# Pooled attention and an eight-expert layer on one core: padded head pairs, values stationary, tokens gathered to expert slots inside SBUF

## The chip, the cores and the metric

One core of a Trainium2 chip runs the whole program. The metric is device time in microseconds (us), the median of several executions. Profiles are of one execution; their times count from the start of its span. All comparisons below use runs of the state "fast" unless a text says otherwise. Engines: PE does matmuls, DVE and ACT are the vector and scalar engines, POOL is the general engine that also gathers and issues casting and indirect DMAs, SP issues plain DMAs.

## The reference, cut to what matters

```python
# q, k, v: (8 batches, 8 heads, 1152, 64) fp32
q_pool = q.reshape(B, H, S // 2, 2, D).mean(axis=3)            # 576 queries per head
attn   = softmax(1 / sqrt(D) * q_pool @ k.T)                   # 576 x 1152 per head
x      = (attn @ v).transpose(0, 2, 1, 3).reshape(4608, 512)   # 4608 tokens
for e in range(8):                                             # each token has one expert
    m = domain_id == e
    out[m] = maximum(x[m] @ w1[e], 0) @ w2[e]                  # 512 -> 1024 -> 512
```

## The kernel before

Heads are done one after the other. Per chunk of 128 keys the scores come out with keys on partitions, go through the exponential, and each 128x128 block of exponentials is then loaded as *weights*, past which 65 columns of values (64 and a column of ones for the softmax sum) are moved. Tokens go to a slot buffer in DRAM (`x_slot`) by indirect DMA and are read back per expert. The listing is shortened, with numbers put in for names.

```python
for c in range(NC + 1):                      # 9 key chunks, software pipelined
    ...
    nc.tensor.matmul(sA, lhsT=klhs, rhs=qrhs[:, 0:320])          # 64 rows
    nc.tensor.matmul(oja[:, 0, :], lhsT=attnT[:, cp, 0:P], rhs=v16[:, cp, :])   # 65 columns
    nc.tensor.matmul(sB, lhsT=klhs, rhs=qrhs[:, 320:576])
    ...
    nc.scalar.activation(attnT[:, c, 0:320], sA, AF.Exp, scale=0.0625)          # L317
    nc.scalar.activation(attnT[:, c, 320:576], sB, AF.Exp, scale=0.0625)        # L318
for jj in range(2, NJ):                      # 27 late value matmuls per head, L323
    for c in range(NC):
        nc.tensor.matmul(tps, lhsT=attnT[:, c, jj*P : jj*P+rows], rhs=v16[:, c, :], ...)
# normalise with ACT (scale = 1/sum) into xrow, then scatter rows to x_slot in DRAM
...
for e in range(E):                           # experts, after all attention
    for tt in range(6):                      # 768 slots per expert
        ...                                  # load 128 tokens, transpose, two layers, scatter
```

The softmax here doesn't subtract the row's maximum and nothing guards it: scores larger than these inputs give would overflow.

## Time and profile before

960.9 us median (960.5 to 962.8, 4 runs).

| stretch of the profile (span 954.4 us) | what happens | granted clock |
|---|---|---|
| 0 to 676 us | attention, a steady head 10.1 us | page: 1.00 to 103 us, then 0.50 (see below) |
| 676 to 697 us | no matmul: the last rows go to DRAM and back | 0.5 |
| 697 to 954 us | experts | about 0.9, with falls to 0.5 |

The first fence has whole lines of the page's head: busy time of each engine with its share of the span, then busy tenths in 40 slices and the granted PE clock in tenths.

```profile
span 954.4 us, 19171 instructions
PE 874.5 (92%) x6793; PEld 457.4 (48%) x6793; DVE 412.6 (43%) x2058; ACT 614.3 (64%) x1916; POOL 151.0 (16%) x183
...
PE   5699999999999999999999999999278898889896
...
ACT  3577677677677776777677776776245655665553
...
PEclk9999655555555555555555555555578998999899
```

PE looks full all through attention, at half the clock. The 1.00 of the first 103 us is no reading: the trace has no clock record before 100.8 us, and sA and sB start 0.24 us apart at 86 us as at 115 us. The groups of instructions (line, engine, operation, shapes, count | busy us, mean ns | idle time of the engine before them and who ended it) show what ACT does there and what it waits for:

```profile
L317 ACT ACTIVATE attnT<-sA 128x320 f16<-128x320 f32 x576 | 254.5, 442 | 164.2 <-PE sA L295 145.6
L318 ACT ACTIVATE attnT<-sB 128x256 f16<-128x256 f32 x576 | 220.7, 384 | 18.2 <-PE sB L307 14.6
L295 PE MATMUL sA<-qT,kT 64*128 64x320 f16 x576 | 226.8, 442 | 0.7 <-ACT attnT L317 0.5
```

The 475 us of exponentials are a floor of that design; ACT idles another 182 us in front of them, mostly for PE, while PE does the late value matmuls, transposes and first scores of the next head. The timeline inside a head shows the two exponentials back to back (start in us, duration in us, instruction, then in brackets the idle time before it and who ended it):

```profile
307.15 0.44 ACT L317 ACTIVATE attnT<-sA 128x320 f16<-128x320 f32 x1 [0.22 <-PE sA L295]
307.49 0.38 ACT L318 ACTIVATE attnT<-sB 128x256 f16<-128x256 f32 x1
```

### The profile page before, as it was taken

The page shows a single profiled execution, that of the slowest core. Times are in us where ns is not written, and L with a number is a line of the kernel's source. Part 1 is how long each engine was busy: PE and PEld are TensorE (multiplying, and loading weights), DVE is VectorE, ACT ScalarE, POOL GpSimd, SP SyncE. Part 2 cuts the span into 40 slices and gives each one's busy share as a digit, 9 for nine tenths or more (in the row PEclk, how much of TensorE's full clock was granted, in tenths as well). Part 3 has the DMA queues.
Part 4 walks back from the last instruction along what each step waited for, and adds up shares of the span by engine and source line. Part 5 has one row for each costly group of instructions (what it writes and reads, how often), then busy time and mean ns, then how long its engine had stood idle before and what let it go on. Part 6 is the DMA issues. An engine that isn't in the chain of part 4 may idle for free. (4 is left out here: it accounts for less than half of the span.)

```text
span 954.4 us, 19171 instructions
## 1 busy us (share of the span) xinstructions
PE 874.5 (92%) x6793; PEld 457.4 (48%) x6793; DVE 412.6 (43%) x2058; ACT 614.3 (64%) x1916; POOL 151.0 (16%) x183
## 2 busy tenths in 40 slices
PE   5699999999999999999999999999278898889896
PEld 1344544444444444444444444444155565556563
DVE  5455554554555554554554554543022312231221
ACT  3577677677677776777677776776245655665553
POOL 8322232220010001002000100200211211221221
PEclk9999655555555555555555555555578998999899
DMA  9964454444345344355363543440025466556221
GB/s 307 302 111 92 97 116 99 95 125 97 79 128 158 82 102 115 91 165 123 77 169 86 121 106 82 120 132 1 25 73 169 155 211 217 163 178 220 64 66 40
DMA packets 230244, 118.31 MB, mean 124 GB/s; under 512 B 169818, under 2 KB 212866, under 8 KB 230148
## 3 DMA queue, kind: packets, MB, share of 16 engines
q1 hardware_dynamic: 221028, 96.61, 38.7%
q0 software_dynamic: 9120, 20.48, 5.9%
q8 instruction: 53, 0.87, 0.4%
q14 instruction: 43, 0.35, 0.1%
HBM read 96.53 MB, written 23.64 MB: 126 GB/s over the span
## 5 line engine op out<-in xcount | busy, mean ns | idle before, releaser
L317 ACT ACTIVATE attnT<-sA 128x320 f16<-128x320 f32 x576 | 254.5, 442 | 164.2 <-PE sA L295 145.6
L318 ACT ACTIVATE attnT<-sB 128x256 f16<-128x256 f32 x576 | 220.7, 384 | 18.2 <-PE sB L307 14.6
L295 PE MATMUL sA<-qT,kT 64*128 64x320 f16 x576 | 226.8, 442 | 0.7 <-ACT attnT L317 0.5
L307 PE MATMUL sB<-qT,kT 64*128 64x256 f16 x576 | 207.2, 406 | 1.5 <-ACT attnT L318 1.1
L265 DVE CAST kT<-tr 128x128 f16<-128x128 f32 (+1 forms) x320 | 85.6, 284 | 178.2 <-PE sB L307 139.2
L405 PE MATMUL hps<-xT,w1h 128*128 128x128 f16 x1536 | 132.7, 228 | 20.6 <-ACT hT L412 13.5
L412 ACT ACTIVATE hT<-hps 128x128 f16<-128x128 f32 x384 | 94.8, 278 | 74.5 <-PE hps L405 71.0
L405 PEld LDWEIGHTS <-w1h 128*128 128x128 f16 x1536 | 110.9, 102 | 62.2 <-issue 55.5
L400 DVE CAST xT<-tpx 128x128 f16<-128x128 f32 x192 | 50.0, 287 | 172.7 <-PE tpx L393 163.2
L298 PEld LDWEIGHTS <-attnT 128*128 128x128 f16 x576 | 56.4, 115 | 132.5 <-ACT attnT L318 113.2
L415 PE MATMUL o_ps<-w2h,hT 128*128 128x512 f16 x384 | 112.8, 397 | 0.0
L323 PEld LDWEIGHTS <-attnT 128*128 128x128 f16 (+1 forms) x1728 | 104.8, 141 | 6.0
L279 DVE CAST qT<-tr 128x128 f16<-128x128 f32 (+1 forms) x320 | 81.5, 271 | 28.9 <-PE tr L272 21.6
L424 POOL DMA_INDIRECT out_dram<-osb,gt x48 | 48.9, 1018 | 207.1 <-ACT hT L412 105.1
L272 PE MATMUL tr<-ident_63,qpa 128*128 128x128 f16 (+1 forms) x320 | 76.2, 269 | 2.0 <-DVE qpa L233 0.6
L295 PEld LDWEIGHTS <-kT 64*128 64x128 f16 x576 | 51.5, 100 | 53.2 <-issue 12.5
L336 DVE RECIPROCAL rec<-oja 128x1 f32<-128x1 f32 (+1 forms) x192 | 30.1, 157 | 105.4 <-PE oja L323 103.8
L309 PEld LDWEIGHTS <-attnT 128*128 128x128 f16 x576 | 60.8, 122 | 21.9 <-PE sA L295 18.7
L227 DVE TENSOR_TENSOR qpa<-q2a 128x64 f16<-128x64 f32 (+1 forms) x320 | 68.9, 215 | 2.2 <-DMA q2a<-in_q_dram 1.9
L307 PEld LDWEIGHTS <-kT 64*128 64x128 f16 x576 | 55.5, 108 | 27.9 <-issue 13.1
L233 DVE TENSOR_TENSOR qpa<-q2a 128x64 f16<-128x64 f32 (+1 forms) x320 | 68.7, 215 | 0.0
L337 ACT ACTIVATE xrow<-oja,rec 128x64 f16<-128x64 f32 (+1 forms) x192 | 61.3, 319 | 3.3 <-DVE rec L336 3.1
(774 smaller groups left out, 939.2 us busy)
## 6 DMA issues: line engine op xcount, KB each, us to landing
w_sb<-in_moe_w_dram SPq DMA_DIRECT2D x16, 2048.0 KB
k_sb<-in_k_dram SPq DMA_DIRECT2D x64, 288.0 KB
v_sb<-in_v_dram SPq DMA_DIRECT2D x64, 288.0 KB
q2a<-in_q_dram SPq DMA_DIRECT2D x256, 64.0 KB
x_slot<-xz_115 POOLq DMA_DIRECT2D x48, 128.0 KB, 4.3
q2a<-in_q_dram SPq DMA_DIRECT2D x64, 32.0 KB
gt<-g_slot SPq DMA_DIRECT2D x48, 0.5 KB
out_dram<-osb,gt POOLq DMA_INDIRECT x48, 2.7
```

Of the source, the lines that this page charges most:

```text
L227: nc.vector.tensor_tensor(out=qpa[0:rows, jj, 0:D], in0=q2a[0:rows, jj, 0:D], in1=q2a[0:rows, jj, D : 2 * D], op=ALU.add,)
L265: nc.vector.tensor_copy(kT[0 : nch * D, p_, :], tps[0 : nch * D, :])
L272: nc.tensor.matmul(tq[:, 0:rows], lhsT=qpa[0:rows, jj, :], rhs=ident16[0:rows, 0:rows], start=True, stop=True,)
L279: nc.vector.tensor_copy(qT[:, jj * P : jj * P + rows], tq[:, 0:rows])
L295: nc.tensor.matmul(sA[:, :], lhsT=klhs, rhs=qrhs[:, 0:NA], start=True, stop=True)
L307: nc.tensor.matmul(sB[:, :], lhsT=klhs, rhs=qrhs[:, NA:Sp], start=True, stop=True)
L317: nc.scalar.activation(attnT[:, c, 0:NA], sA[:, :], AF.Exp, bias=0.0, scale=0.0625)
L318: nc.scalar.activation(attnT[:, c, NA:Sp], sB[:, :], AF.Exp, bias=0.0, scale=0.0625)
L323: nc.tensor.matmul(tps[0:rows, tslot, :], lhsT=attnT[:, c, jj * P : jj * P + rows], rhs=v16[:, c, :], start=(c == 0), stop=(c == NC - 1),)
L405: nc.tensor.matmul(hps[:, :], lhsT=w1h[:, c, f * P : (f + 1) * P], rhs=xT[:, c, :], start=(c == 0), stop=(c == NDc - 1),)
L412: nc.scalar.activation(hT[:, f, :], hps[:, :], AF.Relu)
L415: nc.tensor.matmul(o_ps[:, :], lhsT=hT[:, f, :], rhs=w2h[:, f, :], start=(f == 0), stop=(f == NF - 1),)
```

## The change

The intent: make PE work dense so that the exponentials are the only limit of attention, fill PE's spare time with expert work, and keep tokens inside SBUF.

- Two heads form a pair. Keys of both lie on 128 partitions; the queries of each head are padded with zeros in the other head's 64 rows, so each score matmul has 128 rows.
- Values are the stationary operand, exponentials move (288 columns at a time). The output comes out transposed, x on partitions, ready for the first expert layer. One exponential covers both heads: 576 steps of 576 columns.
- The sums go out by DMA, are inverted, and come back broadcast over partitions; two DVE multiplies per pair normalise into `xT`, 4 channel groups of a token side by side.
- POOL gathers tokens of an expert from `xT` in SBUF (`indirect_copy`). 256 slots per expert ("fill", 128 units on PE, first-half tokens only) run inside the second half of attention, 384 more per expert in a last stage.
- All instruction streams are in an order set by hand.

The diff is a rewrite (746 lines against 461); its core:

```diff
-            nc.tensor.matmul(sA[:, :], lhsT=klhs, rhs=qrhs[:, 0:NA], ...)
-            nc.tensor.matmul(oja[0:P, 0, :], lhsT=attnT[:, cp, 0:P], rhs=v16[:, cp, :], ...)
-            nc.scalar.activation(attnT[:, c, 0:NA], sA[:, :], AF.Exp, bias=0.0, scale=0.0625)
-            nc.scalar.activation(attnT[:, c, NA:Sp], sB[:, :], AF.Exp, bias=0.0, scale=0.0625)
+        for r in range(2):                                   # score(t): step t = (pair, half, chunk)
+            mm(s[:, r, 0:QH], kq[p][:, c * P : (c + 1) * P],
+               qz[p % 2][r][:, hf * QH : (hf + 1) * QH], True, True)
+        nc.scalar.activation(e_[:, :, :], st.pop(t)[:, :, 0:QH], AF.Exp, bias=0.0, scale=0.0625)
+        for head in range(2):                                # av_step(t)
+            mm(acc[u][head][:, 0:QH], v16[p % NV][:, c, P * head : P * head + P],
+               e_[:, head, :], c == 0, c == NC - 1)
+    def norm_c(p, hh):                                       # L469
+        nc.vector.tensor_tensor(
+            out=xT[lo : lo + 64, 1 + b * Sp : 1 + (b + 1) * Sp, hp].rearrange("p (a j) -> p j a", j=NJ),
+            in0=xu[p][hh][lo : lo + 64, :].rearrange("p (j a) -> p j a", j=NJ),
+            in1=srec[p][lo : lo + 64, :].rearrange("p (j a) -> p j a", j=NJ), op=ALU.mult)
+        nc.gpsimd.indirect_copy(                             # gather, L320: 128 tokens x 4 values
+            xs[:, :, j * P : (j + 1) * P].rearrange("p c s -> p s c"),
+            xT[:, 0:hi, :], idx[:, e, t * 8 : (t + 1) * 8], True)
 ... (cut)
+        if main and hf == 0 and c == 0 and p >= 1 and p + 1 < NPAIR:
+            pair_load(p + 1)                                 # k, v by POOL (cast), q by SP
+            if hf == 0 and c == 0:
+                prep_k(p + 1)                                # DVE: kp
+            if hf == 0 and c == 2:
+                burst_k(p + 1)                               # PE: 8 transposes of kp
+            if hf == 1 and c == 6:
+                norm_c(p - 1, 0)
+            if hf == 1 and c == 7:
+                norm_c(p - 1, 1)
```

A pair has 18 steps: two halves (hf) of nine chunks (c).

## The prediction

> **What bounds it now.** The table by stretches shows attention to about 676 us, a 20 us gap without matmuls, experts from 697 to 954. A head takes 10.1 us (oja matmuls): 9 x (442 + 384) ns = 7.4 us is the two exponentials per key chunk, back to back in the timeline; for the other 2.7 us ACT mostly idles (164 us before L317, 146 on PE) while PE does 27 late value matmuls with new weights (1.7 us), transposes and first scores. PE is 100% busy, yet the granted clock is 0.50 from 103 to 700 us. Before that the page says 1.00, but 64x320 matmuls take 442 ns there too, so I read half clock throughout. In the expert stage (0.9 to 1.0) a 128x512 matmul starts every 0.215 us. The Trainium skill ("TensorE: Matmul & The Clock Gate", part 1) has 1.2 GHz idle, 2.4 GHz after sustained activity; this trace shows that a full PE queue of 64-row scores and 65-column value matmuls did not suffice, and that 128x128 expert work raised the clock within about 8 us.
>
> **What changes.** Values become the weights and exp(scores) moves: 576 steps, each two score matmuls (128 rows, half zeros) and two value matmuls of 288 columns, one exponential of 576 columns. Gone: 2880 attnT weight loads, 320 xrow copies (104 us ACT), the x_slot round trip, 8 w2 casts on ACT (29 us). Added: about 40% of the expert work (128 units of 1024 columns) inside attention, 40 gathers and the cast-DMA issues on POOL, a normalisation round trip per pair.
>
> **Costs** (estimates from the trace).
> - Exponential: 0.9 ns per column from 442 and 384 ns, so 576 columns 655 to 670 ns; x576 = 380 us, the floor of attention.
> - PE at full clock, columns/2.4 GHz: 0.49 us per step, transposes about 0.07, a fill unit 0.44. 432 steps without fill are ACT bound, with bursts about 0.70 us: 303. 144 steps with fill are PE bound, about 1.0 us: 145.
> - Dense 128-row work should raise the clock; before's experts kept it at about 68% column activity (8704 columns per 5.3 us tile), the new ACT-bound steps have about 75%.
> - Start 12 us; gap before the tail (normalise, three gathers) 18.
> - Tail: 24,576 columns per expert, 10.3 us. POOL issues three gathers, three scatters (1.0 us each, as before) and for four experts four weight DMAs. No gather is in this trace; I take 2 to 3 us. Then POOL is slightly the limit: 8 x 12 = 96. End 6.
>
> Sum 580; median 585 us, 80% range 530 to 710; faster 0.97, same 0.01, slower 0.02.
>
> **Right if:** ACT over 90% busy until the fill, an exponential about 0.66 us; PEclk near 1.0 from the first tens of us; step time 1.0 us in the fill; PE at 80 to 95% in the tail.
>
> **Wrong if:**
> 1. The clock stays at 0.5 in attention: steps PE bound at 1.05 and 1.9 us, total 750 to 850.
> 2. Gathers are slow. The skill ("GPSIMD Engine Reference", section 7) has about 102 cycles for a small read command per gather index; 128 of them would be an estimated 11 us, 22 us per expert in the fill and 35 in the tail: over 800 us, POOL near 100%.
> 3. PE order makes ACT wait at transposes or late weights.
> 4. DVE, some 13 us per pair in the fill, delays the two shared PSUM buffers.

## The result, and the profile after

906.9 us median (904.3 to 908.9, 4 runs) against 960.9 us. The ratio is 0.943, 95% interval 0.9415 to 0.9453. Ratios in this document are the mean time of one kernel's fast runs over that of the other's of the same rounds, so not quite the ratio of the medians quoted. Faster, by 6% and not by the 39% predicted; the time lies far outside the range.

Names in the views that follow: `s` holds scores, `e` their exponentials, `accA` and `accB` the accumulators of the two heads, `xuA` and `xuB` their copies in SBUF before normalising, `rb` the inverse sums, `kp` the copied keys of the next pair, `mt` the PSUM tile of transposes and fill, `xs` gathered tokens.

The head of the page after. DVE and POOL are given as well here, as they turn out to matter:

```profile
span 902.1 us, 10215 instructions
PE 555.1 (62%) x3619; PEld 360.5 (40%) x3619; DVE 461.9 (51%) x680; ACT 384.9 (43%) x625; POOL 285.2 (32%) x316
...
PE   4787567765786768358358557676860555343555
...
DVE  6867375675767546466465666567662111000111
ACT  3777456745576644135134334674760111100111
POOL 2588210110000042351351331200001456554443
PEclk9999888968798778688687778898895786667887
```

Work fell as planned: PE from 875 to 555 us, ACT from 614 to 385. But no engine is full any more; each waits for others. The groups:

```profile
L420 ACT ACTIVATE e<-s 128x576 f16<-128x576 f32 x576 | 358.6, 650 | 310.0 <-PE s L402 304.0
...
L320 POOL INDIRECT_COPY xs<-xT,idx 128x512 f16 x40 | 112.9, 2823 | 254.1 <-issue 220.4
...
L469 DVE TENSOR_TENSOR xT<-xuA,rb 64x576 f16<-64x576 f32 x32 | 110.1, 3440 | 38.1 <-DMA rb<-s_rec 38.1
...
L469 DVE TENSOR_TENSOR xT<-xuB,rb 64x576 f16<-64x576 f32 x32 | 89.5, 2796 | 1.0
```

One exponential takes 650 ns, close to the 655 to 670 predicted. ACT idles 310 us before them, more than before. Two more things stand out: a multiply of only 576 columns costs 2.8 us, and the gathers have twice as much "issue" before them (220 us) as work (113 us).

The sum of the prediction against the profile. A step is put down to its exponential; the fill is taken as 144 steps from the 313th on, as predicted (in b1, where it starts 12 steps later, from the 325th).

| stretch | predicted us | after, us | with all mends (b1, below), us |
|---|---|---|---|
| start, to the first exponential | 12 | 14.5 | 14.5 |
| 432 steps without fill | 303 | 407.0 | 306.1 |
| 144 steps with fill | 145 | 249.1 | 155.7 |
| last exponential to first matmul of the last stage | 18 | 37.3 | 25.3 |
| last stage and end | 102 | 194.2 | 147.0 |
| sum | 580 | 902.1 | 648.6 |

**A pair without fill** takes 16 to 17 us where it is steady, for 18 x 0.62 = 11.1 us of exponentials. The timeline of DVE around the border of two pairs:

```profile
253.74 2.79 DVE L469 TENSOR_TENSOR xT<-xuA,rb 64x576 f16<-64x576 f32 x1 [0.17 <-DMA rb<-s_rec]
256.56 2.79 DVE L469 TENSOR_TENSOR xT<-xuB,rb 64x576 f16<-64x576 f32 x1
259.38 0.81 DVE L368 COPY kp<-k 128x576 f16<-128x576 f16 x2
260.23 0.46 DVE L443 COPY xuA<-accA 128x288 f32<-128x288 f32 x1
```

and of PE and ACT at the same time:

```profile
256.27 0.29 PE L402 MATMUL accB<-e,v 128*128 128x288 f16 x1
256.39 0.41 PE L402 MATMUL s<-qz,kq 128*128 128x288 f16 x2
260.25 0.62 PE L376 MATMUL mt<-ident,kp 128*128 128x128 f16 x8 [3.45 <-DVE kp L368]
...
261.10 0.45 PE L402 MATMUL accA<-e,v 128*128 128x288 f16 x1
261.34 0.45 PE L402 MATMUL accB<-e,v 128*128 128x288 f16 x1
```

```profile
247.00 10.55 ACT L420 ACTIVATE e<-s 128x576 f16<-128x576 f32 x17 [0.31 <-PE s L402]
261.41 0.65 ACT L420 ACTIVATE e<-s 128x576 f16<-128x576 f32 x1 [3.86 <-PE s L402]
```

Seventeen exponentials run back to back in 10.55 us. Then PE stands at the eight key transposes (L376) for `kp`, which DVE makes only after both multiplies. Scores behind the transposes in PE's order come late, and ACT stops for 3.9 us. A second loss follows: matmuls of 288 columns start 0.12 us apart before the stall and 0.24 us after it, until about 264 us; the clock record has 0.50 from 260.8 to 264.2 us. Each of these steps shows ACT idle 0.31 us. The Trainium skill ("TensorE: Matmul & The Clock Gate", "Why this matters for your kernels") says that idle gaps above about 3 us between bursts send the clock back to half; the trace agrees, with a gap of 3.45 us. Of its 35 falls to half clock, all but the last, at the program's end, have a gap of 3.19 us or more in the 7 us before. It is no sharp bound: in run e7 below, 8 of 22 falls had only gaps of 1.9 to 2.8 us there.

**In the fill**, a pair takes up to 34 us. POOL's timeline there:

```profile
489.99 2.77 POOL L320 INDIRECT_COPY xs<-xT,idx 128x512 f16 x1 [4.21 <-PE s L402]
498.59 2.78 POOL L320 INDIRECT_COPY xs<-xT,idx 128x512 f16 x1 [5.83 <-issue]
500.90 0.84 POOL L90 DMA_DIRECT2D k<-in_k_dram  x1
```

The key load of the next pair stands behind two gathers in POOL's order; it lands at 504.9, and ACT is idle from 496.9 to 507.4 us. ACT's stops in the fill are 6.5 to 16.2 us long. The gathers and the multiplies also slow each other: the multiply that starts at 492.57 us takes 6.28 us in place of 2.79, and these two gathers are 8.6 us apart in place of 6.5. Here it is the part of the gather shown as issue that grows (5.83 us in place of 3.7); the second multiply, beside the part shown as work, keeps its 2.79 us. The skill ("GPSIMD Engine Reference", section 8, "Key points") says that the two engines share SBUF interfaces and that DVE instructions with two SBUF inputs contend; the multiply is one, and the trace agrees.

**In the last stage** an expert takes 26.6 us with weight loads in POOL's order, 23.5 without; PE is busy half of it. One expert on POOL:

```profile
738.14 2.80 POOL L320 INDIRECT_COPY xs<-xT,idx 128x512 f16 x1 [4.15 <-issue]
744.66 2.80 POOL L320 INDIRECT_COPY xs<-xT,idx 128x512 f16 x1 [3.72 <-issue]
751.15 2.82 POOL L320 INDIRECT_COPY xs<-xT,idx 128x512 f16 x1 [3.68 <-issue]
```

Gathers follow each other every 6.5 us although each shows only 2.8 us of work. The 3.7 us of "issue" between them are the engine's own. The skill ("Perfetto Trace Analysis", "GPSIMD Engine Instruction") says that the start shown for such an instruction is a read on its first core and not the start of execution, which fits. Three gathers (19.5 us), three scatters with their memsets (4.0) and four weight issues (3.0) fill the 26.6 us.

### The profile page after: what moved, and what is told of

It is laid out like the page before. It is cut to its first block, busy times and chain, and to the rows that moved or that the text cites. A ratio compares the mean times of both kernels' runs of the same rounds, so it can differ in the third digit from the quotient of the medians.

```text
span 902.1 us, 10215 instructions
## 1 busy us (share of the span) xinstructions
PE 555.1 (62%) x3619; PEld 360.5 (40%) x3619; DVE 461.9 (51%) x680; ACT 384.9 (43%) x625; POOL 285.2 (32%) x316
## 4 chain that ended last, share of the span: by engine, by line
issue 26%; DMA 20%; POOL 19%; DVE 18%; PE 16%; ACT 0%; SPq 0%; POOLq 0%; DVEq 0%; ACTq 0%
POOL xs L320 12%; DVE xT L469 11%; DMA rb<-s_rec 6%; DMA k<-in_k_dram 6%; PE s L402 5%; DMA srow<-xuB 5%; DMA s_rec<-rrow 4%; PE mt L402 3%; POOL g_slot L239 3%; DVE kp L368 2%; PE accA L402 2%; PE accB L402 2%; PE mt L376 2%; PE hp L649 2%; POOL out_dram L329 1%
## 5 line engine op out<-in xcount | busy, mean ns | idle before, releaser
L420 ACT ACTIVATE e<-s 128x576 f16<-128x576 f32 x576 | 358.6, 650 | 310.0 <-PE s L402 304.0
L402 PE MATMUL s<-qz,kq 128*128 128x288 f16 x1152 | 259.8, 310 | 1.7 <-ACT e L420 0.3
L320 POOL INDIRECT_COPY xs<-xT,idx 128x512 f16 x40 | 112.9, 2823 | 254.1 <-issue 220.4
L402 PE MATMUL accA<-e,v 128*128 128x288 f16 x576 | 175.2, 309 | 5.8 <-DVE xuA L443 5.7
L402 PE MATMUL accB<-e,v 128*128 128x288 f16 x576 | 174.3, 307 | 0.3
L376 PE MATMUL mt<-ident,kp 128*128 128x128 f16 x256 | 28.7, 281 | 198.7 <-DVE kp L368 190.6
L402 PEld LDWEIGHTS <-kq 128*128 128x128 f16 x1152 | 118.9, 106 | 79.3 <-issue 34.6
L402 PEld LDWEIGHTS <-v 128*128 128x128 f16 x1152 | 120.8, 105 | 47.4 <-issue 6.8
L469 DVE TENSOR_TENSOR xT<-xuA,rb 64x576 f16<-64x576 f32 x32 | 110.1, 3440 | 38.1 <-DMA rb<-s_rec 38.1
L376 PEld LDWEIGHTS <-kp 128*128 128x128 f16 x256 | 21.3, 126 | 209.6 <-DVE kp L368 201.0
L649 PEld LDWEIGHTS <-w1h 128*128 128x128 f16 x256 | 30.3, 119 | 151.4 <-issue 137.3
L469 DVE TENSOR_TENSOR xT<-xuB,rb 64x576 f16<-64x576 f32 x32 | 89.5, 2796 | 1.0
```

The costliest lines, as they stand in the source:

```text
L320: nc.gpsimd.indirect_copy(xs[:, :, j * P : (j + 1) * P].rearrange("p c s -> p s c"), xT[:, 0:hi, :], idx[:, e, t * 8 : (t + 1) * 8], True,)
L376: nc.tensor.transpose(mt[:, c * P : (c + 1) * P], in_=k16[:, c, :, :].rearrange("p h d -> p (h d)"), identity=ident16[:, :])
L402: nc.tensor.matmul(out_, lhsT=lhsT, rhs=rhs, start=start, stop=stop)
L420: nc.scalar.activation(e_[:, :, :], st.pop(t)[:, :, 0:QH], AF.Exp, bias=0.0, scale=0.0625)
L469: nc.vector.tensor_tensor(out=xT[lo : lo + 64, 1 + b * Sp : 1 + (b + 1) * Sp, hp].rearrange("p (a j) -> p j a", j=NJ), in0=xu[p][hh][lo : ...
L649: nc.tensor.matmul(hp_[:, 0:nsl], lhsT=w1h[:, cc, f * P : (f + 1) * P], rhs=xs[:, cc, 0:nsl], start=cc == 0, stop=cc == ND - 1,)
```

## The experiments

All are edits of the changed kernel unless said otherwise, correct unless said otherwise, and timed in three rounds against the kernel before. Ratios are to the kernel before, as 0.943 is.

### 1. The key transposes later on PE (e1)

```diff
-            if hf == 0 and c == 2:
+            if hf == 1 and c == 0:
                 burst_k(p + 1)
```

> Only the eight key transposes of the next pair move on PE from step 2 to step 9 of a pair (of 18). Theory A: PE waits there for the DVE copy kp, which stands behind the two 2.8 us normalising multiplies on DVE; then the stall of the exponentials of about 4 us at step 2 goes below 1 us, a pair without expert work takes about 12.5 us in place of 16.3, and the whole 770 to 830 us in place of 907. Rival B: the pair is short of PE time or of clock, and the wait only moves to step 9: 880 us or more, with a stall of 3 us or more at the new place.

Measured: 908.0 us, ratio 0.947 [0.943, 0.951]. No gain; theory A in this form fell. The waits (engine, line <- releaser: us in total, times, longest), first of the changed kernel, then of this one:

```profile
ACT e L420 <- PE s L402: 304.0, 213, 16.2
...
PE mt L376 <- DVE kp L368: 190.6, 30, 14.9
```

```profile
ACT e L420 <- PE s L402: 300.5, 250, 15.8
...
PE accA L402 <- DVE xuA L443: 177.5, 31, 14.4
...
PE mt L376 <- DVE kp L368: 10.0, 1, 10.0
```

The wait for `kp` went from 191 to 10 us, and a wait of 178 us (6 before) for the eviction of the accumulators took its place. The time lies in rival B's range, but not by its cause: at the new place of the transposes PE waits once, 10 us. So it is not PE that is short, as rival B had it; both awaited results stand in the same place of DVE's queue, behind the multiplies. Theory A had to be mended: what must move is not the one that waits but what holds DVE.

### 2. The multiply in another element order (e2)

```diff
-            out=xT[...].rearrange("p (a j) -> p j a", j=NJ),
-            in0=xu[p][hh][lo : lo + 64, :].rearrange("p (j a) -> p j a", j=NJ),   # and in1
+            out=xT[...].rearrange("p (a j) -> p a j", j=NJ),
+            in0=xu[p][hh][lo : lo + 64, :].rearrange("p (j a) -> p a j", j=NJ),   # and in1
```

> The normalising multiply visits the same elements in the order of the output (writes 8 bytes apart, reads 384 bytes apart) in place of the order of the input (writes 48 bytes apart, reads in a row); the result is the same. Theory A: the far writes make it cost 2.79 us[...]; it falls to 0.7 to 1.2 us, the stall at step 2 shrinks, 800 to 850 us. Rival B: any scattered 2-byte write costs that, or the far reads cost as much: 2.7 us or more, 890 to 920 us.

Measured: 869.4 us median, but from 853.0 to 874.7, and three of four runs count as slow by that spread, the profiled one too. The size of the gain is left open. The multiply took 1.47 us in place of 2.79: shorter, but not 0.7 to 1.2. The same duration shows again in a fast run, e6 below.

### 3. Scores with 64 rows (e3)

```diff
-                kq[p][:, c * P : (c + 1) * P],
-                qz[p % 2][r][:, hf * QH : (hf + 1) * QH],
+                kq[p][64 * r : 64 * r + 64, c * P : (c + 1) * P],
+                qz[p % 2][r][64 * r : 64 * r + 64, hf * QH : (hf + 1) * QH],
```

> The padding undone: each score matmul takes the 64 rows of its head alone, in place of 128 rows of which half are zeros; the result is the same. Theory A: the rows in use hold the clock up; granted clock falls to about 0.5 in attention, a step gets PE bound at about 1.0 us and the time rises to 930 to 1000 us. Rival B: only the share of time with columns in the array counts: clock and time as in the changed kernel, within 2% of 907. Rival C: matmuls on different row halves overlap, PE time per step falls from 0.49 to about 0.37 us, and as ACT and DVE set the pace the time stays within 3% of 907.

Measured: 916.0 us, ratio 0.959 [0.955, 0.962], which is 1.6% above the changed kernel's 0.943. The mean granted clock is 0.79, as with padding (0.79 to 0.81). The page's line of the clock:

```profile
PEclk9778787778787869797687789897885687667777
```

There is no sign of theory A: the padding of the scores is not what holds the clock up (the value matmuls kept 128 rows). The two scores of a step now start together, but the next value matmul starts 0.23 us after them, as with padding (0.24), so rival C's gain on PE did not come. Padding is worth at most about 1.6% of the time here.

### 4. One gather of three in the last stage (e4, wrong result)

```diff
-        for j in range(R2 // P):
-            gather(xs, j, e, R1 // P + j, N + 1)
+        nc.vector.memset(xs[:, :, P:R2], 0.0)
+        gather(xs, 0, e, R1 // P, N + 1)
```

> Wrong result on purpose: in the last stage one gather of three per expert, the other 256 columns are zeros from a memset on DVE. Theory A: the stage is bound by POOL, where a gather holds the engine 6.5 us (2.8 shown as busy, 3.7 as issue); an expert with weight loads goes from 26.5 us to 12.5 to 14, and the whole to 790 to 815 us. Rival B: late weights or the out writes bind it: 20 us or more per expert, 850 us or more.

Measured: 812.6 us, ratio 0.848 [0.843, 0.853]. Experts with weight loads start 13.5 us apart, those without 10.4: the latter is PE's own time as predicted (10.3 us). POOL binds the stage, mainly by its gathers: the 13.5 us are again its sum, 6.5 for one gather, 4.0 and 3.0. Rival B's late weights or writes do not.

### 5 and 6. The multiplies elsewhere (e5), and reordered as well (e6)

```diff
         if main and p >= 1:
-            if hf == 0 and c == 7:
+            if hf == 1 and c == 0:
                 norm_b(p - 1)
-            if hf == 1 and c == 6:
-                norm_c(p - 1, 0)
-            if hf == 1 and c == 7:
-                norm_c(p - 1, 1)
+        if main and p >= 2:
+            if hf == 0 and c == 3:
+                norm_c(p - 2, 0)
+            if hf == 0 and c == 6:
+                norm_c(p - 2, 1)
-T_FILL = (B // 2 * HP) * 2 * NC + 24
+T_FILL = (B // 2 * HP) * 2 * NC + 36      # those tokens are ready later
```

(After the loop the last but one pair is normalised too.) Run 6 adds the edit of run 2.

> The two normalising multiplies (as slow as in the changed kernel, 2.79 us each) move from the end of a pair to steps 3 and 6 of the pair after, where no PE instruction waits for DVE for some steps; the expert work starts 12 steps later as its tokens are ready later. Theory A, mended after the first run: DVE works in order, and what stands behind the multiplies at the pair boundary (key copy and the eviction of both accumulators alike) stops PE; then the 4 us stall goes below 1 us, a pair without expert work takes 12 to 13.5 us in place of 16.3, the whole 790 to 840 us. Rival B: DVE has too much work in all, the stall reappears elsewhere: a pair over 15 us, 870 us or more.

> As the run before, and with the output order of elements that made the multiply 1.47 us. Theory A: both together leave DVE about 9.5 us of work per pair and no wait at the boundary; a pair without expert work takes 11.5 to 12.5 us, the whole 770 to 815 us. Rival B: as before, over 15 us per pair.

Measured: e5 867.9 us, ratio 0.907 [0.903, 0.911]; e6 810.9 us, ratio 0.847 [0.844, 0.851]. The waits of PE for DVE, of e5 and then of e6:

```profile
ACT e L420 <- PE s L402: 252.7, 202, 13.3
...
PE mt L376 <- DVE kp L368: 76.7, 11, 12.0
...
PE accA L402 <- DVE xuA L443: 41.7, 21, 2.7
```

```profile
ACT e L420 <- PE s L402: 198.3, 183, 13.0
...
PE mt L376 <- DVE kp L368: 75.7, 11, 11.7
...
PE accA L402 <- DVE xuA L443: 11.3, 12, 1.4
```

e5 missed its time (790 to 840 us), though its best pairs fell to 13.4 us as expected: its wait at the accumulators is only smaller, since DVE has little slack with multiplies of 2.79 us (11.2 us of work in 13.4). The multiply of e6 on its page:

```profile
L469 DVE TENSOR_TENSOR xT<-xuA,rb 64x576 f16<-64x576 f32 x32 | 46.9, 1465 | 22.7 <-DMA rb<-s_rec 22.7
```

With it the best pairs take 11.1 us, which is ACT's own time, and the time lies in the expected range. Theory A as mended holds: place and cost of the multiply both matter. One thing is not separated: the move also gives the round trip of the sums 12 steps in place of 8, and DVE's wait for `rb` in front of the multiplies fell from 38.1 us to 19.7 (e5) and 22.7 (e6). In the steady pair shown above that wait is 0.17 us, so it is not the cause there. What is left of the wait for `kp` (76 us in 11 places) is loads that come late: DVE itself waits there for the key load, 67 us in 10 places.

### 7. Loads earlier (e7, on e6)

```diff
-        if main and hf == 0 and c == 0 and p >= 1 and p + 1 < NPAIR:
-            pair_load(p + 1)
+        if main and hf == 0 and c == 6 and p + 2 < NPAIR:
+            pair_load(p + 2)
```

> As the run before, and keys, values and queries of a pair are issued more than a pair earlier. Theory A: in the stretch with expert work the 10 us stall per pair is the key load, which stands in the POOL queue behind two gathers; the period there falls from 28 to 19 to 23 us, the whole 710 to 770 us. Rival B: the gathers themselves (13 to 17 us of POOL per expert) or late weights set that period: 26 us or more, the whole as in the run before within 2%.

Measured: 737.7 us, ratio 0.769 [0.766, 0.773], 73 us below e6 on the same chip. Four fill pairs in a row that took 30.7, 27.7, 29.9 and 27.6 us in e6 take 22.9, 22.9, 20.8 and 21.6 us. PE's wait for `kp` and ACT's for scores:

```profile
ACT e L420 <- PE s L402: 130.0, 177, 12.5
...
PE mt L376 <- DVE kp L368: 15.0, 5, 10.0
```

Theory A holds.

### 8. Gathers of pairs (g1) and one gather of 384 indices (g2)

```diff
-            xs[:, :, j * P : (j + 1) * P].rearrange("p c s -> p s c"),
-            xT[:, 0:hi, :],
+            xs[:, :, j * P : (j + 1) * P, :].bitcast(FP32).rearrange("p c s o -> p s (c o)"),
+            xT[:, 0:hi, :].bitcast(FP32),          # xs is (P, 2, slots, 2); indices times 2 in place of 4
```

```diff
-        for j in range(R2 // P):                   # g2, on g1
-            gather(xs, j, e, R1 // P + j, N + 1)
+        gather(xs, 0, e, R1 // P, N + 1, w=R2)
```

> The changed kernel, but a gather moves the four 2-byte elements of a token as two 4-byte elements (same indices, same bytes; the matmul then reads its moving columns 4 bytes apart). Theory A: a gather costs by the element written (512 of them, 12.7 ns each): 3.2 to 3.8 us in place of 6.5, an expert of the last stage 16 to 18.5 us in place of 26.5 with weight loads, the whole 810 to 850 us. Rival B: it costs by the index (128, 51 ns each): 6 us or more, 890 us or more. Rival C: columns 4 bytes apart halve the matmul rate: the first layer of an expert in the last stage takes 10 us or more of PE in place of 7.3.

> As the run with pairs, whose gather of 128 indices held POOL 4.5 us (0.86 shown busy, 3.66 issue); now the last stage gathers the 384 indices of an expert in one instruction in place of three, the stage with attention keeps gathers of 128. Theory A: the 3.66 us are paid per instruction; the gather of 384 takes 6 to 6.6 us, an expert of the last stage 12 to 14 us in place of 20.5 with weight loads, the whole 770 to 800 us. Rival B: they are paid per index (29 ns each): about 13.5 us for the gather, stage and whole as with pairs, 830 to 850 us.

Measured: g1 841.5 us, ratio 0.879 [0.875, 0.883]; g2 831.1 us, ratio 0.865 [0.860, 0.869]. POOL's timeline in the last stage, of g1 and then of g2:

```profile
707.00 0.86 POOL L320 INDIRECT_COPY xs<-xT,idx 128x256 f32 x1 [3.73 <-issue]
711.52 0.86 POOL L320 INDIRECT_COPY xs<-xT,idx 128x256 f32 x1 [3.66 <-issue]
```

```profile
710.86 1.73 POOL L320 INDIRECT_COPY xs<-xT,idx 128x768 f32 x1 [11.18 <-issue]
```

Neither theory of g1 was right alone. The part that is shown as work fell from 2.8 to 0.86 us with 4-byte elements; the part shown as issue stayed at 3.7 us for 128 indices. Its time lies in the range of theory A (810 to 850), but its gather takes 4.5 us and its expert 20.5, both above A's numbers. g2 then settles the rest for rival B: 384 indices have 11.2 us of issue, so it is paid per index (3.66 / 128 = 28.6 ns; 11.18 / 384 = 29.1 ns) and not per instruction. Rival C of g1 fell: the 32 first-layer matmuls with columns 4 bytes apart take little longer. Where the granted clock is 1.00 all through, the first layer of an expert takes 5.41 us in g1, b1 and b2, from its first matmul to the first of the second layer, against 5.20 us with columns in a row (e4).

### 9. All mends together (b1), and fill spread (b2)

b1 is e7 with the edits of g1 and g2. b2 changes on top:

```diff
-        if T_FILL <= t < NST and t % NC != 1:
+        if T_FILL <= t < NST and t % NC in (0, 2, 4, 6, 8):
```

> Multiplies moved and reordered, loads earlier, gathers as pairs, one gather of 384 per expert. If the gains add: 738 less the 65 us that pairs brought to the changed kernel is 673 us; if one gather of 384 is cheap as well, 610 to 640 us. If they do not add, because the last stage then waits for late weights, over 690 us.

> As the run before, and the 128 units of expert work spread over the whole second half of attention (5 steps of 9 in place of 8 of 9). Theory A: where a unit meets a step PE sets the pace (0.92 us, ACT 30% idle), where none does ACT sets it (0.62 us, PE 20% idle), and in the dense stretch the gathers come too late for the expert; spreading saves 10 to 30 us. Rival B: the sum of PE work is the same and the gathers keep up: within 1% of the run before.

Measured: b1 651.8 us, ratio 0.679 [0.677, 0.680]; b2 642.7 us, ratio 0.669 [0.667, 0.672]. Both are correct, and b2 beats the kernel before by 33% and the changed kernel by 29% (of the medians). b1 took 21 us less than simple addition of e7 and g1 (673), g2's edit included. The spread saved 1.4%, a little below the expected 10 us. The head of b2's page:

```profile
PE 514.4 (81%) x3619; PEld 342.3 (54%) x3619; DVE 350.7 (55%) x680; ACT 378.7 (59%) x625; POOL 201.8 (32%) x300
...
PE   2899796987888997998898898999931947866774
```

With the stalls gone PE is 89 to 93% busy through attention. The last stage still waits for POOL: an expert with weight loads takes 19.7 us.

### 10. The multiply taken apart (n1, wrong result)

```diff
+        if hh == 0:   # writes 8 bytes apart, reads in a row
+            tensor_tensor(out=xT[..., hp], in0=xu[p][hh][lo : lo + 64, :], in1=srec[p][...], op=mult)
+        else:         # reads 384 bytes apart, writes in a row into a scratch
+            tensor_tensor(out=scratch.rearrange("p (a j) -> p a j", j=NJ),
+                          in0=xu[p][hh][...].rearrange("p (j a) -> p a j", j=NJ), in1=..., op=mult)
```

> Wrong result on purpose; only the duration of the two multiplies matters. The multiply of the even head writes 8 bytes apart and reads in a row (tokens permuted); that of the odd head reads 384 bytes apart and writes in a row into a scratch. In the changed kernel both write 48 bytes apart and read in a row (2.79 us); in the reordered one both write 8 bytes apart and read 384 apart (1.47 us). Theory A: far writes are the cost and far reads are not: 1.4 to 1.5 us for the even head, 0.7 to 0.8 for the odd. Rival B: far reads made the rest: 0.7 to 0.8 for the even head, 1.4 to 1.5 for the odd.

Measured: one look, state unknown; only durations are used. The view of `xuA` (least, median and greatest ns), even head first, then odd head:

```profile
L471 DVE TENSOR_TENSOR xT<-xuA,rb x32: 1430/1442/4936, 44.4 to 628.9; 64x576 f16<-64x576 f32 x32
L478 DVE TENSOR_TENSOR xuA<-xuB,rb x32: 1151/1222/1257, 45.9 to 630.3; 64x576 f16<-64x576 f32 x32
```

Medians: even head 1.44 us, odd head 1.22 us. Theory A was right for the even head and wrong for the odd, rival B wrong for both. Writes 8 bytes apart cost 1.44 us by themselves, reads 384 bytes apart 1.22 us, and both in one instruction 1.47 us (e6): the costs do not add. Writes 48 bytes apart cost 2.79 us. A version in which everything lies in a row was not run; the nearest in this trace is a two-input addition of 288 columns in runs of 36, 0.46 us, which gives an estimate of 0.9 us for 576.

## Why the prediction was wrong

- **Right: direction, and what PE and ACT need.** The exponential takes 650 ns (655 to 670 predicted), back to back 0.62 us. A fill step at PE's pace takes 0.92 us (about 1.0), an expert of the last stage with POOL out of the way 10.4 us (10.3). With the stalls mended (b1) the 432 steps without fill take 306 us and the 144 with fill 156, near the 303 and 145 of the sum. That the 306 comes so close is partly luck: steady pairs of b1 take 11.1 us (0.62 per step, 268 in all), and others still wait (12 to 17.6 us).
- **Right: the clock rises.** The first doubt, half clock throughout attention, did not come true: the granted clock is 0.81 in the mean, matmuls of 288 columns start every 0.12 us. It is not the "near 1.0" of the prediction, and the clock record has 35 falls to 0.50. And "dense 128-row work should raise the clock" is not borne out as a reason: with scores of 64 rows it held as well (e3), though the values kept 128; density was not tested. Why the kernel before stays at half clock with PE in work all the time is not settled by these runs.
- **Wrong step: "432 steps without fill are ACT bound, with bursts about 0.70 us: 303".** It took 407. The sum had ACT and PE but no DVE in these steps. The third doubt named ACT waiting at the transposes, but with PE's order as the cause and no cost; e1 showed that their place on PE is not it. DVE stood only in the fourth doubt, for the fill, as total work. What stopped the steps was not DVE's total (11.5 us of work in a pair of 17) but its order: two multiplies of 2.79 us just ahead of two results that PE awaits within two steps. Their cost was the second half of the miss: the prediction gave them no number at all. e1 showed that moving one of the two waiting instructions is useless, e5 and e6 that moving and shortening the multiplies removes the stall. Not all of the 104 us above the sum is theirs: these steps take 346 us in e6 and, with loads earlier, 323 in e7, so 61 went with the multiplies and 24 with late loads.
- **Wrong step: "144 steps with fill are PE bound, about 1.0 us: 145".** It took 249. ACT stopped 6.5 to 16.2 us in each pair, with the key load behind two gathers on POOL. The third doubt ("late weights") looked in that direction, but at the wrong load. e7 showed it, and brought 73 us in all, 46 of them in these steps (220 us in e6, 173 in e7); e6 had taken 29 before (its multiplies take 1.5 us in the fill, none 6.3), and the cheaper gathers of b1 take 18 more.
- **Mis-sized term: "I take 2 to 3 us" for a gather.** It is 6.5 us: 3.7 for 128 indices and 2.8 of shown work for 512 two-byte elements (0.86 for the same bytes as 256 four-byte elements, g1). The second doubt's estimate from the skill, 11 us, erred the other way. The last stage became 194 us in place of 102, and the gap before it 37 us in place of 18: it holds three gathers in a row, 20 us from the end of the last multiply (687.8) to the first matmul (707.9). The form of the term, POOL as the limit of the last stage, was right (e4).
- **Where the expected gain went.** Of the 322 us between sum and profile, 104 are steps without fill, 104 steps with fill, 19 the gap and 92 the last stage (rest: 2.5 at the start). They are new waits on the two engines that the change made into suppliers, DVE and POOL, while the two engines that the prediction counted got their gain.

## What to carry to other kernels

When a rewrite empties the busiest engines, cost the engines that now feed them as carefully, and not by total work but by order: list what stands ahead of each result that an in-order engine awaits within a step or two. Removing one wait of several that have the same holder moves the time to the next wait; move or shorten the holder. An operation of which no trace exists (here the gather) deserves a range as wide as its doubt, and the strides of small elements, read or written, belong in the price: the same 576 columns cost 2.79 or 1.47 us here, by their order alone.

## What the Trainium skill lacked or had wrong

- "GPSIMD Engine Reference", section 7: about 102 cycles (85 ns at the page's 1.2 GHz) for a small read command per gather index. The figure does not carry over to this gather: it costs 28.6 to 29.1 ns per index (g1, g2), a third of that, and besides 2.8 us of shown work for 512 two-byte elements or 0.86 us for the same bytes as 256 four-byte elements. No page has a cost for this instruction.
- "Vector Engine (DVE) Microarchitecture Reference", section 5.2, has times for strides of 4-byte elements, but none for 2-byte writes. Here a multiply of 64x576 took 2.79 us with 2-byte writes 48 bytes apart and 1.44 us with 2-byte writes 8 bytes apart (n1).
- "GPSIMD Engine Reference", "Key points", names the contention with DVE but no size, and "SBUF — State Buffer" has none for a gather beside a multiply: here a multiply went from 2.79 to 6.28 us, and gathers from 6.5 to 8.6 us apart, when both ran.
- "TensorE: Matmul & The Clock Gate", part 1: sustained activity gives full clock. In the kernel before PE is 100% busy by the profile's windows for hundreds of us at a granted 0.50. What counts as activity is not told, but for a word on transposes in part 4; scores of 64 rows in place of 128 changed nothing (0.79 against 0.79 to 0.81, e3).
